# Mean of values for keyless queries in a hash attention: from GpSimd sums and a late addition to TensorE sums and one matmul per head

## The chip, the cores and the metric

The kernel runs on one core of a Trainium2 chip. The metric is the time of one execution on the device, in microseconds, as the median of several runs. The core's engines are TensorE (PE), VectorE (DVE), ScalarE (ACT), GpSimd (POOL) and SyncE (SP), which here mainly issues DMAs. Each engine runs its own instructions strictly in the order in which they stand for it.

## What is computed

Attention over hash buckets comes first: 2 batches of 8 heads, 768 queries and keys, 64 columns per head. A query attends only to the keys whose 6-bit hash equals its own. Where a query has no key in its bucket, all its scores are equal, so its result is the plain mean of all 768 values of the head. The result feeds a mixture of 8 experts.

```python
mask = q_bucket[:, :, :, None] == k_bucket[:, :, None, :]
scores = scale * np.matmul(q, k.transpose(0, 1, 3, 2))
scores = np.where(mask, scores, -1000000000.0)
scores = scores - np.max(scores, axis=-1, keepdims=True)
attn = np.exp(scores)
attn = attn / (np.sum(attn, axis=-1, keepdims=True) + 1e-09)
return np.matmul(attn, v)
...
x = attn_out as (1536, 512); logits = x @ w_gate; one expert per row, capacity 384
out[i] = gate_w[i] * (relu(x[i] @ w1[e]) @ w2[e])
```

## The kernel before

A table named ORDER lists some 900 short steps, written out by hand. The kernel runs them one after the other, each issuing a few instructions, so the table fixes the order on every engine. A step's name may carry an engine after a colon (`:a` ScalarE, `:v` VectorE, `:p` GpSimd, `:vp` one of two each).

The 16 heads (batch times 8 plus head) are handled in two manners. For an **even** head, steps `dS dM dX dY dE d1 f1 f2 dv dw dP dR dQ dN` work on 24 groups of two query tiles: scores on PE (`dS`), the row maximum on DVE (`dM`), its sign and scale (`dX`, `dY`), the exponential on ACT (`dE`), the split into a high and a low part in f16 (`d1` ACT, `dv` DVE and `dw` POOL), a transposing DMA from SP (`f1`, `f2`), the product with the values on PE (`dP`), and the division on DVE (`dR dQ dN`). For an **odd** head, steps `rM rR rF` find all row maxima, `mT mA mD` transpose them and write them by DMA into two rows of the query operand `QB`, and then `rS rE r1 r2 rP` form transposed scores, exponentials, the two parts and the product, three steps per head. The odd head's product accumulates in a PSUM tile of tag `acc`, and `fs` divides it into X.

PSUM tags: `pt` score tiles, `acc` (one buffer), `misc` (one buffer, shared by `mt`, `vb`, `dacc` and others).

Values come in four groups `w` of four heads (HV = 4); a group holds two odd heads. Step `va` takes the largest absolute value, `vT vR vE vB vC` make a power-of-two scale of it on all partitions (`vB` on PE, `vC` on DVE), `v1` writes the high part in f16 with a column of ones beside it, and `v2` the low part.

The mean of an odd head goes another way: `vS` adds the six tiles of raw values on POOL (line 334 once, line 336 four times per group), `vB` sums over partitions with a matmul by ones in f32 (line 977), `vA` copies it, scaled by 1/768, to SBUF on ACT (line 991). `rF` has POOL mark the queries without a key (line 296, `nm`), `nm` multiplies mark and mean (line 401) on POOL or DVE, and `fa` adds that to X after `fs` (line 908).

Of the kernel before, what the change touches and what calls it, by code (L numbers as in the profile page):

```python
# [63 lines left out]
dE1.0 rR3.0 rM4.1 vA1 pl5 rS2.1 vC1 r10 v20.1 rM5.1 rE2.1 v10.2:a dP2 rR5.1 pl2 f10 rM4.0 rM5.0 rR4.1 rS1.1 dR2
v11.3:a v11.0:a rR4.0 dQ2 rR5.0 v20.2 rS1.0 r20:pp rS2.0 pb5 d11 f20 rE1.1 dN2 v21.3 sH7:a pb2 rM3.1 rE1.0 dP0 dS3.0
dv1:v rE2.0 dR0 rR3.1 dQ0 ph4 ph7 dS3.1 sL7 rP0 dw1:p dM3.0 f11 r11 rM8.0 v11.1:a f21 dX3.0 ld6 rF3 dY3.0:a dM3.1 dN0
r21:pp r12 dX3.1 rR8.0 hM2.0 hB2.0 dE3.0 rM7.0 r22:pp rR7.0 dS5.0 dY3.1:a dS4.1 dE3.1 dM5.0 mT3 d13 dS5.1 rP1 mA3
dv3:p dM5.1 hM2.1 dM4.1 dX5.0 dX5.1 f13 mD3 dX4.1 v11.2:a rP2 hB2.1 dY5.1:a dP1 dY5.0:v dw3:v pl4 v21.2 v20.3 dE5.1
pl7 f23 dE5.0 fs1 pb4 rS3.0 v21.0 dR1 dY4.1:a dQ1 dE4.1 fa1:p rE3.0 rS3.1 rM6.1 rR6.1 d15 rE3.1 rM7.1 rM8.1 dN1 rR7.1
rS5.0 dS4.0 rR8.1 dw5:p lT0.0.0 r13 rM6.0 dv5:v rE5.0 dM4.0 lC0.0.0:a dS7.0 dX4.0 dP3 rR6.0 dY4.0:a dE4.0 rS4.1 r23:vp  # L70
dR3 rS5.1 ld9 dQ3 f15 f25 ww2 tb v21.1 pb7 d14 dN3 dM7.0 f14 rE4.1 dX7.0 lM0.0.0 rF5 rE5.1 lv2 lA0.0.0 dw4:p sH6:a
rS4.0 nm3:v lT0.0.1 dv4:v dS7.1 dY7.0:v rE4.0 dM7.1 dX7.1 dS6.1 lC0.0.1:a mT5 sH9:a mA5 dY7.1:v r14 f24 rP3 dM6.1 dP5
dX6.1 dY6.1:v dE7.0 dE7.1 dS6.0 sL6 dR5 dQ5 mD5 d17 dN5 dM6.0 ph6 sL9 hM3.0 dX6.0 r15 r24:pv f17 rS6.0 ld11 dw7:v
# [13 lines left out]
lC0.2.1:a dw12:p dS14.0 nm7:v lM0.2.0 dv12:p mD9 dM13.1 dE13.0 r111 lA0.2.0 dM14.0 ph13 dS14.1 hM5.0 dX13.1 dY13.1:a
rP10 dX14.0 dE13.1 dM14.1 rM16.1 hB5.0 dP11 dX14.1 rR16.1 dR11 dY14.0:a f112 pl13 dQ11 dN11 dE14.0 v22.1 dY14.1:a
v22.2 r211:pp f212 rS12.0 rS13.1 d113 vT3 pl10 pb13 dE14.1 rE12.0 rS12.1 vR3 rP11 rE12.1 dw13:v f113 r112 dv13:p dP12
ld12 pb10 rM18.1 dR12 rS13.0 rE13.1 vE3 d114 dQ12 sH12:a rM15.1 dN12 rR18.1 vB3 f213 rR15.1 rS14.1 vA3 rE13.0 dS15.1  # L90
vC3 r212:pp lM0.2.1 ld15 fs7 wm dM15.1 lA0.2.1 ph12 rS14.0 dP13 dv14:v v13.3:a rE14.1 f114 rM19.0 dR13 dQ13 sL12 rE14.0
sH15:a dw14:p wF dX15.1 dN13 sL15 dY15.1:a dS15.0 rF11 r113 rR19.0 dE15.1 f214 dM15.0 mT11 rP12 mA11 dX15.0 dS17.0
dY15.0:a hM6.1 fa7:v dS17.1 dM17.0 dE15.0 dX17.0 r213:pp hB6.1 d115 r114 dM17.1 rM20.0 hM6.0 rR20.0 dX17.1 dS16.1
hB6.0 dv15:p mD11 ph15 dY17.0:a dY17.1:a dE17.0 lT0.3.1 rP13 lC0.3.1:a v13.1:a dM16.1 dw15:v lT0.3.0 rM19.1 f115
dE17.1 dX16.1 dY16.1:a v22.3 v23.3 r214:vv f215 lC0.3.0:a rS16.0 dP14 vO3 rE16.0 dR14 pl12 dQ14 rS16.1 nm9:v dN14 d117
# [1485 lines left out]
```

## Time and profile before

| What | us |
|---|---|
| Median of three runs (424.79, 429.37, 437.17) | 429.37 |
| The profiled execution | 425.73 |
| Span from first to last instruction in its trace | 423.9 |

The profiled execution is 3.64 us below the median of the runs, and 1.8 us of it lie outside the span. A time worked out from the trace is therefore added to 425.73 and compared with that first. Attention takes the first 250 us or so, the experts most of the rest.

### The profile page before, as it was taken

To read this page: it belongs to the slowest core of one execution; us is meant where nothing else is said; L and a number is where in the kernel's file an instruction comes from. 1 tells how busy PE (TensorE), PEld (TensorE's weight loads), DVE (VectorE), ACT (ScalarE), POOL (GpSimd) and SP (SyncE) were. 2 spreads that over 40 slices of the span, in tenths; PEclk is the share of its full clock that TensorE was granted. 3 is DMA by queue.
4 is the path that set the end of the run, shared out by engine and by line. 5 is a ranking of instruction groups with operands and counts; after the bars stand their busy time and mean duration, and the time that the engine had idled before them with its cause. 6 is when DMAs were issued, how large, how long until landed. Compare 5 with 4: busy or idle time off the path is not lost.

```text
span 423.9 us, 10033 instructions
## 1 busy us (share of the span) xinstructions
PE 392.8 (93%) x3839; PEld 307.0 (72%) x3839; DVE 324.0 (76%) x773; ACT 301.2 (71%) x412; POOL 210.1 (50%) x194
## 2 busy tenths in 40 slices
...
PEclk9999799999999996999999998999999999999998
...
GB/s 205 262 221 133 162 180 168 243 233 180 220 185 191 177 156 208 145 187 226 177 195 207 123 338 275 231 347 359 365 340 286 260 321 283 310 252 46 37 4 38
DMA packets 112400, 89.84 MB, mean 212 GB/s; under 512 B 92226, under 2 KB 94258, under 8 KB 112344
## 3 DMA queue, kind: packets, MB, share of 16 engines
...
q8 instruction: 32, 0.52, 0.5%
...
HBM read 48.37 MB, written 6.88 MB: 130 GB/s over the span
## 4 chain that ended last, share of the span: by engine, by line
issue 32%; PE 22%; DVE 15%; DMA 12%; POOL 8%; ACT 6%; SPq 3%; POOLq 1%; another core or an unknown queue 0%; ACTq 0%; DVEq 0%
PE pt L713 12%; DVE dm L727 4%; PE dacc L791 4%; DMA t<-d 3%; POOL xr L184 3%; DMA QB<-mr 2%; DMA xd<-X 2%; DVE mx L831 2%; POOL y L1352 2%; DVE d L780 2%; ACT p L758 2%; ACT p L862 2%; DMA KB<-bits 2%; PE acc L791 2%; DMA xr<-xd,gix 1%
## 5 line engine op out<-in xcount | busy, mean ns | idle before, releaser
L1352 POOL DMA_INDIRECT y<-y,yix x16 | 18.5, 1158 | 121.1 <-ACT y L1351 110.8
L780 POOL TENSOR_TENSOR p<-p,p 128x768 f16<-128x768 f32 x37 | 63.1, 1726 | 18.2 <-ACT p L866 12.0
L1342 PE MATMUL ph<-x,w1h 128*128 128x224 f16 x448 | 64.9, 259 | 0.0
L713 PE MATMUL pt<-KA,QA 128*128 128x512 f32 x192 | 57.5, 382 | 2.1 <-ACT p L862 0.9
L780 POOL TENSOR_TENSOR d<-p,d 128x768 f16<-128x768 f32 x27 | 46.7, 1740 | 23.0 <-ACT d L766 12.2
L1342 PE MATMUL ph<-x,w1l 128*128 128x224 f16 x224 | 58.1, 259 | 0.0
L713 PE MATMUL pt<-KB,QB 78*128 78x512 f32 x192 | 53.0, 359 | 4.0 <-DMA KB<-bits 1.8
L1260 DVE SCALAR_TENSOR_TENSOR w2l<-r,wsc,w2h 128x1024 f16<-128x1024 f32 x28 | 35.6, 1280 | 25.9 <-ACT w2h L1279 25.9
L831 DVE TENSOR_REDUCE mx<-pt 128x1 f32<-128x768 f32 x48 | 45.0, 951 | 8.5 <-PE pt L713 8.1
L862 ACT ACTIVATE p<-pt,lnb 128x768 f32<-128x768 f32 x48 | 42.4, 894 | 9.1 <-PE pt L713 5.6
L758 ACT ACTIVATE p<-pt,ds 128x768 f32<-128x768 f32 x48 | 46.9, 987 | 2.2 <-POOL d L780 0.5
L727 DVE TENSOR_REDUCE dm<-pt 128x1 f32<-128x768 f32 x48 | 45.3, 948 | 2.7 <-PE pt L713 2.5
L1373 PEld LDWEIGHTS <-hh 128*128 128x128 f16 (+1 forms) x256 | 28.1, 110 | 25.9 <-issue 1.1
L1342 PEld LDWEIGHTS <-w1h 128*128 128x128 f16 x448 | 43.4, 98 | 1.5
L1373 PE MATMUL py<-w2h,hl 128*128 128x512 f16 (+1 forms) x112 | 42.5, 379 | 0.0
L1373 PE MATMUL py<-w2l,hh 128*128 128x512 f16 (+1 forms) x112 | 42.5, 379 | 0.0
L1373 PE MATMUL py<-w2h,hh 128*128 128x512 f16 (+1 forms) x112 | 42.5, 379 | 0.0
L1260 DVE SCALAR_TENSOR_TENSOR w1l<-r,wsc,w1h 128x1024 f16<-128x1024 f32 x28 | 35.9, 1284 | 7.2 <-ACT w1h L1270 7.1
L1305 ACT ACTIVATE hh<-ph 128x224 f16<-128x224 f32 (+2 forms) x69 | 23.0, 341 | 22.7 <-PE ph L1342 20.2
L713 PEld LDWEIGHTS pt<-KB,QB 78*128 78x128 f32 x192 | 31.7, 203 | 10.2 <-DMA QB<-bits 4.5
L766 ACT ACTIVATE d<-p 128x1536 f16<-128x1536 f32 x24 | 35.5, 1480 | 5.0 <-DMA t<-d 2.9
L713 PEld LDWEIGHTS pt<-KA,QA 128*128 128x128 f32 x192 | 31.9, 204 | 8.6 <-ACT p L862 2.1
...
## 6 DMA issues: line engine op xcount, KB each, us to landing
...
```

The lines of the kernel that those rows point to most:

```text
L713: nc.tensor.matmul(t[:, a:z], s[:K, q * 128:(q + 1) * 128], m[:K, a:z], start=(n == 0), stop=(n == 1))
L727: nc.vector.tensor_reduce(out=m, in_=tiles["d", k, t][:, 0:S], axis=AX.X, op=ALU.max, negate=True)
L758: nc.scalar.activation(out=p32_of("dp", k)[:, t], in_=pt_last("d", k, t), func=AF.Exp, scale=s[:, 0:1], bias=s[:, 1:2])
L766: nc.scalar.activation(out=tiles["d1", k], in_=tiles["dp", k], func=AF.Copy)
L780: eng.tensor_tensor(out=out[:, t], in0=p32[:, t], in1=p1[:, t], op=ALU.subtract)
L791: nc.tensor.matmul(a[:, 0:c], p, v, start=first and n == 0, stop=last and n == 2, skip_group_check=True)
L831: nc.vector.tensor_reduce(out=m[:, 0, q:q + 1], in_=pt_last("m", r, t), axis=AX.X, op=ALU.max)
L862: nc.scalar.activation(out=p32_of("rp", r)[:, t], in_=pt_last("e", r, t), func=AF.Exp, scale=0.125, bias=lnb)
L1260: nc.vector.scalar_tensor_tensor(out=lo, in0=r, scalar=sc, in1=hi, op0=ALU.mult, op1=ALU.subtract, accum_out=chk_col())
L1342: nc.tensor.matmul(ph, w[:, k], x2[:, 4 * a + k], start=(n == 0), stop=(n == 11))
L1352: nc.gpsimd.indirect_dma_start(out=view, out_offset=bass.IndirectOffsetOnAxis(ap=yix[:m, j:j + 1], axis=0), in_=y[:m], in_offset=None, bou ...
L1373: nc.tensor.matmul(py[t], h[:, g, c], W2[e, g][w], start=(f == 0 and n == 0), stop=(f == 7 and n == len(ops) - 1))
```

## The change

The four steps `vS`, `vA`, `nm`, `fa`, the second matmul of `vB` and the marking in `rF` go. In their place:

- `uM` (per group): twelve f16 matmuls add the high and low parts of the values of the two odd heads over all 768 keys, with a stationary operand of 12 equal columns, into the `acc` bank (12 rows, 130 columns). `uB` copies that to f16 on ACT, `uK` subtracts this copy from rows 6 to 11 by one matmul, so that they hold the rest, and `uL` spreads the rows on DVE into `sel`, 12 rows by 780 columns, zero wherever the row is not that of the query tile.
- `mN` (per odd head): DVE makes `none`, 12 rows by 128 queries, 32768 where a query has no key and 0 elsewhere, out of the transposed maxima, right behind `mA`. The `misc` buffer is held until then.
- The first `rP` of each odd head starts with one matmul of `none` by `sel` (390 columns), to which the products with the values are then added; `fs` divides all of it.

In the table, `v20.3` and `v21.3` change places, as do `v22.2` and `v22.3`, and `rP18` moves from behind `f218` to behind `dS21.0`. Line numbers of the changed kernel are larger by 13 to 15 in these parts.

```diff
-sH5:a rR2.1 ph2 zp0 rR1.1 vS0 dS2.1 dM2.1 rF1 dS2.0 dX2.1 dM2.0 dS0.1 dX2.0 sL5 dY2.1:a mT1 mA1 vB0 dM0.1 dE2.1
+sH5:a rR2.1 ph2 zp0 rR1.1 dS2.1 dM2.1 rF1 dS2.0 dX2.1 dM2.0 dS0.1 dX2.0 sL5 dY2.1:a mT1 mA1 mN1 vB0 dM0.1 dE2.1
...
-            nc.gpsimd.tensor_scalar(out=nm, in0=mx[g][:, 0], scalar1=-BIG / 2, scalar2=None, op0=ALU.is_lt)
...
-        def v_mean(w):
-            t = vv[w, "raw"].rearrange("p (h a) k d -> p h a k d", a=2)[:, :, 1]
-            a = big.tile([128, HV // 2, D], F32, tag="vsum", name="vsum")
-            nc.gpsimd.tensor_tensor(out=a, in0=t[:, :, 0], in1=t[:, :, 1], op=ALU.add)
-            for k in range(2, NT):
-                nc.gpsimd.tensor_tensor(out=a, in0=a, in1=t[:, :, k], op=ALU.add)
-            vv[w, "sum"] = a
...
-            on().tensor_tensor(out=tmp, in0=nmat.pop(g).unsqueeze(2).to_broadcast([128, NT, D]),
-                                    in1=vv[w, "mean"][:, h // 2:h // 2 + 1].to_broadcast([128, NT, D]), op=ALU.mult)
...
+        def mean_sums(w):
+            if w == 0:
+                mean_const()
+            mean[w] = m = ps.tile([128, NT, D + 1], F32, tag="acc", name="ms")[0:12, 0:HR]
+            for n, x in enumerate(("v1", "v2")):
+                v = vv[w, x].rearrange("p (h a) k d -> p a h k d", a=2)[:, 1]
+                for k in range(NT):
+                    nc.tensor.matmul(m[:, :, 0:D + 1 - n], c12, v[:, :, k], start=(n == 0 and k == 0), stop=False,
+                                     skip_group_check=True)
+
+        def mean_high(w):
+            nc.scalar.activation(out=mb, in_=mean[w], func=AF.Copy)
+
+        def mean_low(w):
+            nc.tensor.matmul(mean[w], d12, mb, start=False, stop=True, skip_group_check=True)
+
+        def mean_rows(w):
+            shape = [12, HR, NT, D + 1]
+            nc.vector.tensor_tensor(out=sel, in0=mean.pop(w).unsqueeze(2).to_broadcast(shape),
+                                    in1=em.unsqueeze(1).unsqueeze(3).to_broadcast(shape), op=ALU.mult)
...
+            def mN(g):
+                none[g] = rot.tile([12, 128], F16, tag="nt", name="nt", bufs=3)
+                nc.vector.tensor_scalar(out=none[g], in0=tiles.pop(("mt", g))[:12, :128], scalar1=-BIG / 2, scalar2=32768.0,
+                                        op0=ALU.is_lt, op1=ALU.mult)
...
+                if r % 3 == 0:
+                    nc.tensor.matmul(a.rearrange("p t d -> p (t d)"), none.pop(g), sel[:, h // 2].rearrange("p t d -> p (t d)"),
+                                     start=True, stop=False, skip_group_check=True)
...
-            def fa(g):
-                b, h = divmod(g, H)
-                xo = X[:, b * NT:(b + 1) * NT, h * D:(h + 1) * D]
-                on().tensor_tensor(out=xo, in0=xo, in1=nmts.pop(g), op=ALU.add)
```

VectorE near 52 us in the trace of before: `v21.3` (line 328, a low part of values of group 1), then `dv1` (line 780), then `dR0` (line 811, which reads the PSUM tile `dacc`).

```order
L821 TENSOR_TENSOR X<-dacc,rsd 128x2x64
L328 SCALAR_TENSOR_TENSOR v_537<-vraw_281,scs,v_536 128x384
L780 TENSOR_TENSOR d_688<-p_516,d_629 128x768
L811 TENSOR_SCALAR rsd<-dacc,scs 128x2
L831 TENSOR_REDUCE mx<-pt 128x1
```

The same place after the change; `v_376` and `v_377` are the two parts of the values of group 0.

```order
L836 TENSOR_TENSOR X<-dacc,rsd 128x2x64
L325 SCALAR_TENSOR_TENSOR v_377<-vraw_234,scs,v_376 128x384
L395 TENSOR_SCALAR d_130<-cs 12x12
L397 TENSOR_TENSOR em<-cs 12x6
L795 TENSOR_TENSOR d_691<-p_503,d_614 128x768
L417 TENSOR_TENSOR sel<-ms,em 12x780
L826 TENSOR_SCALAR rsd<-dacc,scs 128x2
L846 TENSOR_REDUCE mx<-pt 128x1
```

`v20.3` has taken the place of `v21.3`, and two small constants and the spreading into `sel` (`uL0`, line 417) now stand ahead of `dR0`.

Group 2 on ScalarE, near 160 us: the copy of the mean (`vA3`, line 991), then exponentials of odd heads (line 862: `rE13.0`, `rE14.1`, `rE14.0`) and a high part of the values (`v13.3`, line 322).

```order
L686 ACTIVATE KA_111<-raw_2619 128x768
L991 ACTIVATE mean<-vb 128x128
L862 ACTIVATE p_2636<-pt,lnb 128x768
L322 ACTIVATE v_2679<-vraw_1657,scs 128x6x64
L862 ACTIVATE p_2747<-pt,lnb 128x768 x2
L686 ACTIVATE KA_114<-raw_2688 128x768
```

The same place after the change.

```order
L701 ACTIVATE KA_111<-raw_2619 128x768
L882 ACTIVATE p_2636<-pt,lnb 128x768
L410 ACTIVATE mb<-ms 12x130
L319 ACTIVATE v_2676<-vraw_1669,scs 128x6x64
L882 ACTIVATE p_2758<-pt,lnb 128x768 x2
L701 ACTIVATE KA_114<-raw_2685 128x768
```

The copy for the mean has moved from ahead of `rE13.0` to behind it, and it reads `ms`, the sums of `uM2`.

Group 2 on TensorE, a little further on: scores `rM19.0`, scores `dS15.0`, the transposed maxima `mT11` (line 842) and the first product of `rP12`.

```order
L713 MATMUL pt<-KB_123,QB_118 128x512
L713 MATMUL pt<-KB_123,QB_118 128x256
L713 MATMUL pt<-KA_112,QA_107 128x512
L713 MATMUL pt<-KA_112,QA_107 128x256
L713 MATMUL pt<-KB_122,QB_117 128x512
L713 MATMUL pt<-KB_122,QB_117 128x256
L842 MATMUL mt<-cs,mx 12x128
L791 LDWEIGHTS p_2579
```

The same place after the change.

```order
L728 MATMUL pt<-KB_123,QB_118 128x512
L728 MATMUL pt<-KB_123,QB_118 128x256
L413 LDWEIGHTS d_130
L413 MATMUL ms<-mb,d_130 12x130
L728 MATMUL pt<-KA_112,QA_107 128x512
L728 MATMUL pt<-KA_112,QA_107 128x256
L728 MATMUL pt<-KB_122,QB_117 128x512
L728 MATMUL pt<-KB_122,QB_117 128x256
L857 MATMUL mt<-cs,mx 12x128
L907 LDWEIGHTS nt
L907 MATMUL acc<-sel,nt 128x390
L806 LDWEIGHTS p_2579
```

`uK2` stands between the two score steps and needs ScalarE's copy, and the product of `none` and `sel` now opens `rP12`.

## Rows read from the trace of the kernel before

**Rows 1.** The page: engine, busy us (share of the span) xinstructions, then clock by slice

```profile
PE 392.8 (93%) x3839; PEld 307.0 (72%) x3839; DVE 324.0 (76%) x773; ACT 301.2 (71%) x412; POOL 210.1 (50%) x194
...
PEclk9999799999999996999999998999999999999998
```

**Rows 2.** Windows: us, busy time (xinstructions) of PE, PEld, DVE, ACT, POOL, clock, DMA share

```profile
75.00:100.00 25.00, 23.84 (x311) 20.02 (x310) 23.39 (x48) 23.49 (x28) 19.78 (x15) 1.00 1.11 227
275.00:300.00 25.00, 25.00 (x180) 17.75 (x178) 21.10 (x53) 19.33 (x28) 6.77 (x4) 1.00 1.07 356
```

**Rows 3.** Groups by shape, removed work: line engine op out<-in xcount | busy us, mean ns

```profile
L336 POOL TENSOR_TENSOR vsum<-vsum,vraw 128x128 f32<-128x128 f32 x16 | 8.0, 503 | 1.3
...
L908 POOL TENSOR_TENSOR X<-X,nmt 128x384 f32<-128x384 f32 x5 | 5.3, 1063 | 10.5 <-DVE X L902 10.5
...
L401 POOL TENSOR_TENSOR nmt<-nm,mean 128x384 f32<-128x384 f32 x5 | 4.1, 826 | 0.0
...
L908 DVE TENSOR_TENSOR X<-X,nmt 128x384 f32<-128x384 f32 x3 | 2.8, 942 | 0.0
...
L401 DVE TENSOR_TENSOR nmt<-nm,mean 128x384 f32<-128x384 f32 x3 | 2.4, 814 | 0.0
...
L977 PE MATMUL vb<-vsum,cs 128*128 128x128 f32 x8 | 2.0, 326 | 0.0
...
L991 ACT ACTIVATE mean<-vb 128x128 f32<-128x128 f32 x4 | 1.0, 260 | 0.0
```

**Rows 4.** Groups by shape again, operations like those that are added

```profile
L821 DVE TENSOR_TENSOR X<-dacc,rsd 128x128 f32<-128x128 f32 x24 | 6.9, 287 | 0.4
...
L902 DVE TENSOR_TENSOR X<-acc,rsr 128x384 f32<-128x384 f32 x8 | 4.5, 558 | 0.3
...
L850 DVE SCALAR_TENSOR_TENSOR mr<-mt,mh 12x128 fp32r<-12x128 f32 x8 | 2.2, 278 | 0.3
```

**Rows 5.** Timeline near 52 us: start, us, engine, line, op, out<-in xcount [idle before <-releaser]

```profile
51.78 0.52 PE L713 MATMUL pt<-KA,QA 128*128 128x512 f32 x2
...
52.09 0.95 DVE L780 TENSOR_TENSOR d<-p,d 128x768 f16<-128x768 f32 x1
...
52.49 1.27 PE L791 MATMUL dacc<-v,t 128*128 128x65 f16 x36
...
53.80 0.22 DVE L811 TENSOR_SCALAR rsd<-dacc,scs 128x2 f32<-128x2 f32 x1 [0.77 <-PE dacc L791]
```

**Rows 6.** Chain that ended last, near 63 us: start us, us, what

```profile
63.15 4.29 DMA QB<-mr
```

**Rows 7.** The chain near 105 and near 220 us

```profile
105.52 4.40 DMA KB<-bits
...
218.08 1.00 POOL X L908
...
220.30 4.39 DMA t<-d
```

**Rows 8.** Windows of 2 us near 160 us

```profile
158.00:160.00 2.00, 0.81 (x6) 0.47 (x4) 0.00 (x0) 0.98 (x2) 0.35 (x1) 1.00 0.36 79
160.00:162.00 2.00, 1.96 (x9) 1.61 (x9) 1.55 (x6) 2.00 (x5) 1.73 (x1) 0.59 1.03 199
162.00:164.00 2.00, 2.00 (x17) 1.60 (x17) 2.00 (x3) 0.87 (x2) 1.83 (x3) 0.50 0.98 277
```

**Rows 9.** Timeline near 162 us

```profile
160.38 0.16 DVE L982 COPY scs<-vb 128x4 f32<-128x4 f32 x1 [2.43 <-ACT mean L991]
...
161.03 0.61 ACT L322 ACTIVATE v<-vraw,scs 128x384 f16<-128x384 f32 x1
...
162.25 1.64 POOL L780 TENSOR_TENSOR d<-p,d 128x768 f16<-128x768 f32 x1 [0.17 <-POOL QB L931]
...
162.44 2.27 DVE L780 TENSOR_TENSOR d<-p,d 128x768 f16<-128x768 f32 x1
...
163.57 0.90 ACT L862 ACTIVATE p<-pt,lnb 128x768 f32<-128x768 f32 x1 [1.13 <-PE pt L713]
```

More of the change, by code (lines that the diff above doesn't have):

```diff
@@ L64 @@
[L64 to L73, printed above, removed]
@@ new lines @@
+dY2.0:a dE2.0 dS0.0 ph3 d12 vC0 hM1.1 ph5 dX0.1 dS1.1 dY0.1:v ld7 mD1 dM0.0 ld4 v10.0:a dX0.0 f12 hB1.1 vO0 hM0.1
+dE0.1 dY0.0:a dw2:p dE0.0 rS0.0 v10.1:a hB0.1 hM0.0 rE0.0 dv2:p va1 dS1.0 hB0.0 rS0.1 vT1 sH4:a dM1.1 pl3 rE0.1 sL4
+f22 vR1 v10.3:a d10 dM1.0 dX1.1 vE1 pb3 hM1.0 hB1.0 dv0:p vB1 dY1.1:a rM3.0 dX1.0 v20.0 dY1.0:a dE1.1 dw0:v dE1.0
+rR3.0 rM4.1 pl5 rS2.1 vC1 r10 v20.1 rM5.1 rE2.1 v10.2:a dP2 rR5.1 pl2 f10 rM4.0 rM5.0 rR4.1 rS1.1 dR2 v11.3:a v11.0:a
+rR4.0 dQ2 rR5.0 v20.2 rS1.0 r20:pp rS2.0 pb5 d11 f20 rE1.1 dN2 v20.3 sH7:a pb2 uM0 rM3.1 uB0 rE1.0 dP0 uK0 dS3.0 dv1:v
@@ new lines @@
+uL0 rE2.0 dR0 rR3.1 dQ0 ph4 ph7 dS3.1 sL7 rP0 dw1:p dM3.0 f11 r11 rM8.0 v11.1:a f21 dX3.0 ld6 rF3 dY3.0:a dM3.1 dN0
+r21:pp r12 dX3.1 rR8.0 hM2.0 hB2.0 dE3.0 rM7.0 r22:pp rR7.0 dS5.0 dY3.1:a dS4.1 dE3.1 dM5.0 mT3 d13 dS5.1 rP1 mA3 mN3
+dv3:p dM5.1 hM2.1 dM4.1 dX5.0 dX5.1 f13 mD3 dX4.1 v11.2:a rP2 hB2.1 dY5.1:a dP1 dY5.0:v dw3:v pl4 v21.2 v21.3 dE5.1
+pl7 f23 dE5.0 fs1 pb4 rS3.0 v21.0 dR1 dY4.1:a dQ1 dE4.1 rE3.0 rS3.1 rM6.1 rR6.1 d15 rE3.1 rM7.1 rM8.1 dN1 rR7.1 rS5.0
+dS4.0 rR8.1 dw5:p lT0.0.0 r13 rM6.0 dv5:v rE5.0 dM4.0 lC0.0.0:a dS7.0 dX4.0 dP3 rR6.0 dY4.0:a dE4.0 rS4.1 r23:vp dR3
@@ L87 @@
[L87 to L95, printed above, removed]
-ld14 rP14 lM0.3.0 v23.1 rE16.1 pl15 rS15.0 rR19.1 lA0.3.0 lM0.3.1 v13.0:a dE16.1 pb12 fs9 rS15.1 dw17:v fa9:v r116
+mN9 dX12.1 dY12.1:a dM13.0 rM15.0 rR15.0 dX13.0 hM5.1 r210:pp dE12.1 d112 dS13.1 dY13.0:a hB5.1 ph10 lT0.2.1 f211
```

117 lines of the change are left out of this document (64 added, 53 removed).

## The prediction

> **What bounds the kernel now.** I read the page first. TensorE is busy for 392.8 of 423.9 us, 93%, VectorE for 76%, GpSimd for 50% [rows 1]. The windows by stage then separate two kernels. In the experts, from 275 us on, TensorE is busy for 25.00 of 25 us; nothing that the change touches runs there, except that it may start later. In attention, 75 to 100 us, TensorE has 23.84, VectorE 23.39 and GpSimd 19.78 us of 25 [rows 2]: three engines that hand work to each other in a fixed order, with one to six us of slack each. So a busy us saved on GpSimd, the one with most slack, is not a us saved, while a us put in the order of TensorE or VectorE is one unless a transfer is waited for later on. Third, the chain that ended last: it passes through DMAs of 4.3 to 4.4 us (maxima into `QB` at 63.15, hash bits into `KB` at 105.52, transposed parts at 220.30) [rows 6, 7]. Behind such a DMA a delay stays only if it was there before the DMA was issued.
>
> **What goes.** On GpSimd: 8.0 us of sums (line 336), 5.3 of `fa`, 4.1 of `nm` [rows 3], 17.4 us in the three largest groups of an engine that is idle for half the span. On VectorE 2.8 + 2.4 = 5.2 us, on TensorE 2.0, on ScalarE 1.0 us [rows 3]. What is worth something of that:
> - VectorE's three heads of 1.76 us each (0.94 + 0.81). Most stand where TensorE or ScalarE end nearly as late; I take half of one pair, 0.9 us, between 0 and 5.2.
> - `vC3` on VectorE waits 2.43 us for ScalarE's `vA3` [rows 9], since both read the bank that `vB3` wrote. That wait goes. But right behind it TensorE has been waiting for a DMA (busy 0.81 us of the 2 from 158 on) [rows 8], and that stays. I take 0.3, between 0 and 0.9.
> - GpSimd's `fa11` stands on the chain at 218.08 for 1.00 us, and behind it is the issue of the transposing DMA at 220.30 [rows 7]. By the table SP has another transposing DMA (`f120`) and a weight load (`wp0`) to issue ahead of that one, whatever GpSimd does: 0.
> - Fewer moments in which VectorE and GpSimd run together. At 162.44 VectorE's product takes 2.27 us while GpSimd's stands at 162.25 for 1.64 [rows 9], and the same instruction takes 0.95 us at 52.09 [rows 5]. The 17.4 us would have to meet VectorE in an instruction that is slowed, on the chain. I take 1.0, from 0 to 7 (a third of the 17.4 us, and the 1.32 us that this one instruction lost).
>
> **What comes, in each odd head.** `mN` reads 12 x 128 like line 850, 0.28 us each [rows 4], so 2.2 us on VectorE for eight, behind `mA` and ahead of row maxima that wait. The matmul of `none` by `sel` has 390 columns. The 36 matmuls of a product, 2328 columns of the same width of data, take 1.27 us [rows 5], 0.55 ns per column, so 0.21 us, or 1.7 us for eight. `rP` on TensorE has little to wait for, so most of the 1.7 delays TensorE, but only a part of both lies where the chain runs. Together 3.9 us, of which I take 1.0; bounds 0 and 3.9.
>
> **What comes, in each group.** `uM` has 1548 columns in twelve matmuls, by the same price 0.84 us at full clock. `uB` is like `vA`, 0.26 [rows 3]. `uK` is one matmul of 130 columns, 0.1 us. `uL` makes 780 columns out of PSUM: lines 821 and 902 take 287 ns for 128 and 558 for 384 columns [rows 4], 1.06 ns a column and 0.15 at the start, so 0.98 us. The work by itself is 1.9 us a group, 7.6 us in all. Worse is that the four are a chain across PE, ACT, PE and DVE, each with other work queued behind it.
>
> *Group 0, near 52 us.* `uM0` waits for `v20.3`, which VectorE ends just ahead of 52.09, while TensorE is free for it at 51.78, where it starts `rM3.1` in before [rows 5]: 0.3 to 0.4 us of wait. So TensorE is late by 0.4 + 0.84 = 1.2 us when `dP0` (52.49 in [rows 5]) starts. `uK0` is queued behind `dP0` and `uL0` on VectorE behind `uK0`; `dR0`, which VectorE ran at 53.80 as soon as `dP0` ended [rows 5], comes after 1.2 + 0.1 + 0.98, 2.3 us late. All of VectorE is behind it: `rR3.1`, `dX3`, `dN0`, and the maxima that go ahead of the DMA at 63.15 [rows 6]. This lies before the issue, so it stays. I take 2.3; the least is 0.8 (if slack on the way takes TensorE's wait and half of the spreading), the most 2.8.
>
> *Group 1, near 99 us.* VectorE spreads for 0.98 us and no longer runs one `fa` and `nm` pair of 1.76; TensorE gets 0.9 us more. At 105.52 the chain goes over to a 4.40 us DMA for hash bits [rows 7], for which TensorE waits whatever came before. I take 0.1, from 0 to 0.9.
>
> *Group 2, near 162 us.* The clock granted here is half: 0.59 and 0.50 in the windows from 160 and 162, after the wait in which TensorE is busy for 0.81 us of 2 [rows 8]. `uM2` stands behind `rS14.0` and takes 1.7 us rather than 0.84. `uB2` stands on ScalarE ahead of `v13.3` and two exponentials, the last of which runs at 163.57 for 0.90 us, right behind the end of `rS14.0` [rows 9]. It can't start until `uM2` ends, near 163.5 + 1.7 = 165.2, so that ScalarE ends at 165.2 + 0.26 + 0.61 + 2 times 0.90 = 167.9, 3.4 us late. `rM19.0` waits for the bank that they free, `uK2` for `rM19.0`, `uL2` for `uK2`, and on VectorE a sign and scale (`dX15.1`) waits for `uL2`, 4.2 us late if nothing is absorbed. Some is, since the stretch is loose with the clock at half. I take 2.8, from 1.5 to 4.2.
>
> *Group 3, near 216 us.* `uL3` and `mN15` (0.98 + 0.28) stand ahead of `dM22.0`, and `rP18` moves back by one score step, so that TensorE doesn't wait for `sel`. The DMA at 220.30 follows an SP queue that is full, and is waited for to 224.69 [rows 7]. I take 0.8, from 0 to 1.5.
>
> **The sum.** Added: 2.3 + 0.1 + 2.8 + 0.8 + 1.0 = 7.0. Gone: 0.9 + 0.3 + 1.0 = 2.2. Net +4.8 us, 430.5 for an execution like the profiled one at 425.73. The median of the three runs is 3.64 above the profiled one and the lowest 0.9 below it; between them, with a third of the distance, the forecast is 431. A measurement of this kernel can tell some 2% from no change, 8.5 us; the forecast lies inside that.
>
> **Rivals.**
>
> *GpSimd's relief decides (faster).* The place is all of attention: 17.4 us less on GpSimd, and with them the slowed VectorE instructions go and GpSimd's products (lines 780) start earlier. For it: the 2.27 us against 0.95 [rows 9, 5]. Against it: GpSimd is idle half of the time [rows 1], and the transfers behind its products are issued by SP in order. With the 7 us bound for the relief, the rest of the gains at their upper bounds (5.2 + 0.9) and 7.0 added, the sum is -6.1: 420. It takes over if a third of the removed GpSimd time is met by VectorE.
> [...]
>
> *The chain of four steps drops the clock (slower).* TensorE waits near 52 us for `uM0`, and near 165 us for the bank behind `uB2`. If those waits lower its granted clock as the wait at 158 to 160 us did, to 0.50 for about 6 us [rows 8], each costs some 3 us more, as half of 6; two of the 40 slices show such a fall in before [rows 1]. With 4.2 for group 2, 2.8 for group 0 and 2 times 3: 7.0 + 1.4 + 0.5 + 6.0 - 2.2 = +12.7, 438. It decides from a wait of about 1.2 us on TensorE, as the 158 us one was; group 0's is 0.4, and group 2 is at half clock already, so one of the two drops at most is likelier: 434 to 436.
>
> *Nothing is left over (same).* The three 4.3 us DMAs [rows 6, 7] and SP's queue absorb all but what is ahead of the first one. Then +2.3 from group 0 and less than the gains from the rest: 426 to 428. For it: behind each such DMA TensorE waits for its landing; against it: the delays in groups 0 and 2 come before the issue of the next DMA.
>
> *The change does not take its work off GpSimd* can be ruled out: its steps are no longer in the table.
>
> **How the numbers follow.** My forecast, some 3 to 8 us more, has 0.50; nothing left over 0.22; the clock or a longer chain 0.18; relief 0.10. The range reaches from the relief case's upper half, 422, to 440, one above the clock case with 438. Faster by over 2% needs 8.5 us, more than the relief case's 6.1 gives from the median: 0.07 with what I can't see. Slower by over 2% needs the clock case or both bounds, 0.18. Within 2%: 0.75.
>
> **What would show it.** GpSimd's busy time about 188, VectorE's within 2 us of 324, TensorE's 395 or more at the same clock. At 52 us `dR0` should run about 2.3 us later than 53.80, and the DMA at 63.15 by about the same. At 162 us `uM2` at 1.7 us, `uB2` ending near 165.5, and the exponential of 163.57 near 167. The 2.43 us wait of `vC3` should be gone. I am wrong if the DMA at 63.15 starts no later, if the slowed VectorE products become rare, or if a window of half clock appears near 53 us or ends later than 168 us.

## The result, and the profile after

The changed kernel takes 433.72 us (median of 20 runs, 429.87 to 443.32); the kernel before took 427.32 us in the runs beside it (20 runs). The ratio is 1.0138, 95% interval 1.0108 to 1.0169: slower by 6 us, inside 2%. Some executions of each kernel are longer (of the changed one four of the 20, 436.54 to 443.32 us); the ratios leave these out, the medians do not, and the profiles of `e2_sums`, `e3_again` and `e3_hybrid`, which are such executions, are not used. The profiled execution took 433.79 us, its span is 432.0, 8.1 us more than that of before.

The page of the changed kernel: busy time by engine, then the granted clock in 40 slices.

```profile
PE 397.4 (92%) x3891; PEld 309.5 (72%) x3891; DVE 326.9 (76%) x781; ACT 302.4 (70%) x412; POOL 189.8 (44%) x157
...
PEclk8568999989999999899999999999999999999998
```

GpSimd has lost 20.3 us of work against [rows 1], VectorE has gained 2.9 and TensorE 4.6. The gain on VectorE is not added work: in a second profile of this kernel (`e1_again` below) VectorE is busy for 322.2 us, 1.8 less than in before. The clock row is new too: the low slices stand at the start now.

The windows of the stages that stood in [rows 2] (time, then busy time of PE, PEld, DVE, ACT, POOL).

```profile
75.00:100.00 25.00, 20.91 (x282) 17.17 (x282) 22.07 (x40) 20.36 (x23) 15.83 (x11) 0.93 0.96 215
275.00:300.00 25.00, 23.76 (x198) 18.83 (x197) 22.29 (x70) 19.53 (x35) 6.93 (x4) 1.00 1.05 320
```

From 75 to 100 us TensorE is busy for 20.91 us of 25 where it was for 23.84. None of the added steps explains this loss; the reason comes below.

The groups by shape of the added operations.

```profile
L417 DVE TENSOR_TENSOR sel<-ms,em 12x780 f16<-12x780 f32 x4 | 3.8, 956 | 2.9 <-PE ms L413 2.8
...
L907 PE MATMUL acc<-sel,nt 12*128 12x390 f16 x8 | 2.8, 354 | 0.0
...
L870 DVE TENSOR_SCALAR nt<-mt 12x128 f16<-12x128 f32 x8 | 2.2, 269 | 0.0
L406 PE MATMUL ms<-v,c 128*12 128x130 f16 x24 | 2.1, 220 | 0.0
L406 PE MATMUL ms<-v,c 128*12 128x128 f16 x24 | 2.0, 220 | 0.0
...
L410 ACT ACTIVATE mb<-ms 12x130 f16<-12x130 f32 x4 | 1.1, 269 | 4.8 <-PE ms L406 4.8
...
L413 PE MATMUL ms<-mb,d 12*12 12x130 f16 x4 | 0.9, 216 | 0.4 <-ACT mb L410 0.4
```

The spreading takes 0.956 us (forecast 0.98), the marks 0.269 (0.28), the copy 0.269 (0.26). The records of matmuls overlap: one of `uM` is 0.22 us long, and twelve in a row take 0.86 us (forecast 0.84), as the next rows show. So the 0.354 us of the product of `none` are not its price either: the next matmul starts 0.26 us after it at 54.48 (forecast 0.21).

The timeline of the changed kernel at group 0, near 50 us.

```profile
49.93 0.86 PE L406 MATMUL ms<-v,c 128*12 128x130 f16 x12
...
50.82 0.27 ACT L410 ACTIVATE mb<-ms 12x130 f16<-12x130 f32 x1 [0.29 <-PE ms L406]
...
52.73 0.22 PE L413 MATMUL ms<-mb,d 12*12 12x130 f16 x1
...
52.98 0.96 DVE L417 TENSOR_TENSOR sel<-ms,em 12x780 f16<-12x780 f32 x1 [1.68 <-PE ms L413]
...
53.87 0.20 DVE L826 TENSOR_SCALAR rsd<-dacc,scs 128x2 f32<-128x2 f32 x1
...
62.95 0.79 SPq L874 DMA_DIRECT2D QB<-mr  x1
```

`uM0` takes 0.86 us, `uK0` stands behind `dP0`, VectorE waits 1.68 us for it and spreads for 0.96, and `dR0` runs at 53.87. By the absolute time this is as late as in [rows 5] (53.80), but the changed kernel had come to this place 1.94 us ahead (before's clock was granted at 0.50 from 42 to 46 us), so `dR0` lost 2.0 us. The DMA that stood at 63.15 in [rows 6] starts at 62.95, so it lost 1.7.

The timeline at group 2.

```profile
164.07 0.15 DVE L989 COPY scs<-vb 128x4 f32<-128x4 f32 x1
...
166.69 0.85 PE L406 MATMUL ms<-v,c 128*12 128x130 f16 x12
...
167.58 0.27 ACT L410 ACTIVATE mb<-ms 12x130 f16<-12x130 f32 x1 [2.03 <-PE ms L406]
...
168.26 1.66 ACT L882 ACTIVATE p<-pt,lnb 128x768 f32<-128x768 f32 x2
...
170.33 0.96 DVE L417 TENSOR_TENSOR sel<-ms,em 12x780 f16<-12x780 f32 x1 [1.12 <-PE ms L413]
...
171.22 0.13 DVE L747 TENSOR_SCALAR ds<-dm 128x1 f32<-128x1 f32 x1
```

`vC3`, which waited 2.43 us in [rows 9], waits for nothing. `uM2` runs at full clock, in 0.85 us and not 1.7. ScalarE waits 2.03 us for it.

To place the losses I took the start of each TensorE step in one profile less its start in the profile of before (for `lM0.2.1` that of its fourth matmul of six), and from that how much later the step at the far side of a place is than the one at its near side. These are worked out from the timelines, in us.

| Kernel (profiled execution) | group 0, `rS2.0` to `rM8.0` | group 1, `rM9.0` to `rM12.0` | group 2, `lM0.2.1` to `hM6.1` | group 3, `dS22.0` to `rS21.1` | sum | near 89, `rS6.1` to `rM11.0` | last product |
|---|---|---|---|---|---|---|---|
| changed, first profile | 1.60 | 1.36 | 1.77 | 1.87 | 6.60 | 4.93 | 255.6 |
| changed, `e1_again` | 1.60 | 1.34 | 1.78 | 1.86 | 6.58 | 0.04 | 251.2 |
| `e1_removed`, no mean | 0.01 | 0.30 | -0.95 | 0.01 | -0.63 | -0.01 | 246.6 |
| `e2_move` | 0.01 | -0.20 | -0.88 | 0.26 | -0.81 | 1.39 | 248.9 |
| `e2_none` | 0.37 | 0.18 | -1.86 | 0.84 | -0.47 | 1.53 | 246.5 |
| `e1_chain` | 1.25 | 1.01 | 0.11 | 1.51 | 3.88 | 0.00 | 251.8 |
| `e3_half` | 1.26 | 1.01 | 1.63 | 1.54 | 5.44 | 1.54 | 251.2 |
| `e2_twice` | 2.29 | 2.05 | 3.23 | 2.55 | 10.12 | 5.14 | 261.8 |
| `e1_late` | 2.01 | 1.35 | 2.18 | 1.86 | 7.40 | 1.50 | 255.3 |
| `e4_fill` | 1.60 | 1.36 | 1.86 | 1.88 | 6.70 | 1.37 | 254.8 |

The last column is the end of the last attention product from the span's start; in before it is 246.9. Both profiles of the changed kernel lose the same 6.6 us at the four groups. Only the first loses 4.93 near 89 us.

Two cautions. In group 2 before runs at half clock [rows 8], so a number there is a difference of two clocks too; counted from the first matmul of `lM0.2.1` it is lower by 0.4 us (by 0.2 in `e3_half` and `e2_twice`). And at `rS2.0`, ahead of group 0, all these kernels stand 1.1 to 3.9 us ahead of before. Much of that lead is gone by the end: `e1_removed` is 3.92 us ahead at `rS2.0` and 0.3 at the last product. So the sum of the four places is what is lost there and not the difference of the ends.

### The profile page after: what moved, and what is told of

It is laid out like the page before. It is cut to its first block, busy times and chain, and to the rows that moved or that the text cites. A ratio compares the mean times of both kernels' runs of the same rounds, so it can differ in the third digit from the quotient of the medians.

```text
span 432.0 us, 10111 instructions
## 1 busy us (share of the span) xinstructions
PE 397.4 (92%) x3891; PEld 309.5 (72%) x3891; DVE 326.9 (76%) x781; ACT 302.4 (70%) x412; POOL 189.8 (44%) x157
## 4 chain that ended last, share of the span: by engine, by line
PE 33%; issue 29%; DVE 14%; DMA 13%; POOL 5%; ACT 4%; SPq 1%; POOLq 1%; another core or an unknown queue 0%; DVEq 0%; ACTq 0%
PE pt L728 15%; PE dacc L806 4%; DMA t<-d 4%; PE acc L806 4%; DVE dm L742 3%; POOL xr L184 3%; DVE d L795 3%; PE pb L272 2%; DMA xd<-X 2%; DMA xr<-xd,gix 2%; DVE mx L846 2%; POOL y L1366 1%; ACT p L882 1%; PE ph L1356 1%; PE py L1387 1%
## 5 line engine op out<-in xcount | busy, mean ns | idle before, releaser
L795 POOL TENSOR_TENSOR p<-p,p 128x768 f16<-128x768 f32 x37 | 62.0, 1692 | 30.1 <-ACT p L886 17.5
L795 POOL TENSOR_TENSOR d<-p,d 128x768 f16<-128x768 f32 x27 | 49.2, 1835 | 44.8 <-DMA t<-d 32.1
L728 PE MATMUL pt<-KA,QA 128*128 128x512 f32 x192 | 58.8, 390 | 2.9 <-ACT p L882 1.6
```

Of the source, the lines that this page charges most:

```text
L728: nc.tensor.matmul(t[:, a:z], s[:K, q * 128:(q + 1) * 128], m[:K, a:z], start=(n == 0), stop=(n == 1))
L795: eng.tensor_tensor(out=out[:, t], in0=p32[:, t], in1=p1[:, t], op=ALU.subtract)
```

## The experiments

The theories: A, the added steps stand ahead of other work on TensorE, ScalarE and VectorE (A1: TensorE's time for the sums by itself; A2: the waits along the four steps), and B, the changed timing makes VectorE's and GpSimd's two-operand products meet. All ratios are to before, run on the same chip, with 95% intervals.

**e1_again.** The changed kernel, unchanged, for a second profile.

> The changed kernel once more, for a second profile. Theory A (queues: the added steps stand ahead of other work on TensorE, ScalarE and VectorE, and that is the loss): the time is 1.2 to 1.6% over before, and the four places are late as in the first profile, by about 1 us near 52, 0 to 2.5 near 165 and 2 near 220. Theory B (meeting: the changed timing lets two-operand products of VectorE and GpSimd meet near 88 to 92 us, where VectorE's two take 4.7 us rather than 1.9): the 3.3 us jump near 89 us stands in this profile too. If the jump is missing and the time is the same, the jump was one execution's chance.

431.7 us, ratio 1.0048 (0.999 to 1.0106), below the 1.2 to 1.6% that theory A expected. The four places are late as in the first profile, and the jump near 89 us is missing. The rows on both sides of it, in the first profile:

```profile
87.62 3.95 POOL L795 TENSOR_TENSOR p<-p,p 128x768 f16<-128x768 f32 x2 [0.69 <-POOL p L795]
87.67 4.72 DVE L795 TENSOR_TENSOR d<-p,d 128x768 f16<-128x768 f32 x2
...
93.03 1.17 PE L272 MATMUL pb<-KA,ST 128*56 128x384 f32 x4 [3.17 <-DVE bits L281]
```

and in the second:

```profile
86.56 1.82 DVE L795 TENSOR_TENSOR d<-p,d 128x768 f16<-128x768 f32 x2
...
87.41 4.11 POOL L795 TENSOR_TENSOR p<-p,p 128x768 f16<-128x768 f32 x2 [2.66 <-issue]
```

In the first, GpSimd's two products (`r25`) start at 87.62, VectorE's two (`dw7`, `dv7`) at 87.67; VectorE then takes 4.72 us and TensorE waits 3.17 us for hash bits behind it. In the second VectorE's first product starts 0.85 us ahead of GpSimd's, and its two take 1.82. That order alone doesn't decide: in `e1_late` VectorE's first is ahead by 0.82 us too, and the two take 3.3. There it is VectorE's second product that meets GpSimd's first one:

```profile
86.67 1.65 POOL L795 TENSOR_TENSOR p<-p,p 128x768 f16<-128x768 f32 x1 [2.65 <-issue]
86.72 2.42 DVE L795 TENSOR_TENSOR d<-p,d 128x768 f16<-128x768 f32 x1
```

The same two in `e1_chain`:

```profile
88.29 0.95 DVE L794 TENSOR_TENSOR d<-p,d 128x768 f16<-128x768 f32 x1
88.34 2.42 POOL L794 TENSOR_TENSOR p<-p,p 128x768 f16<-128x768 f32 x1 [2.60 <-issue]
```

With 0.05 us between the starts, the one that starts second takes 2.42 us, and the other 0.95 (VectorE) or 1.65 (GpSimd). In the first profile above VectorE's products start 0.05 us behind GpSimd's, and the two take 4.72 us. But in `e1_again` GpSimd's product starts first by the records, 0.02 us ahead (87.41, VectorE's second at 87.44), and is the slow one with 2.49 us. What slows one of the two is not shown.

It is a race that goes either way: VectorE's two products take 1.8 us in before, `e1_removed`, `e1_again` and `e1_chain`, and 3.3 to 3.5 in `e1_late`, `e2_move`, `e2_none`, `e3_half`, `e4_fill` and `e2_twice`, so both outcomes come with the change and without it. The 4.72 us came in one profile alone, and whether the change makes the bad outcome likelier is not shown. Theory B fell as an account of what the four groups lose: that is the same with the jump and without it.

**e1_removed.** Before, with the mean of values left out altogether: two of the lines that go are below, and from the table go `vS0` to `vS3`, `vA0` to `vA3` and every `nm` and `fa`.

```diff
-            nc.gpsimd.tensor_scalar(out=nm, in0=mx[g][:, 0], scalar1=-BIG / 2, scalar2=None, op0=ALU.is_lt)
...
-                nc.tensor.matmul(t[:, 128:128 + n_mean], cs[:, C_ONE:C_ONE + 128], ...
...
```

> The kernel before, with the mean of values left out altogether: no sums on GpSimd, no second matmul of vB, no copy, no marks, no product and no addition to X; nothing is added and no step is moved. Theory A: what was taken away is worth 2.2 us (0 to 4), so 423 to 427 where before is 427.3, -0.5%. Theory B: the same work removed shifts GpSimd, so that this kernel is no faster or even slower than before by up to 3 us, with a jump near 89 us. If GpSimd's relief were worth a lot, it would be 7 us or more faster.

429.64 us, ratio 0.9998 (0.9931 to 1.0064). No gain shows from all that the change takes away: without it, and with nothing put in its place, the time is that of before, to within 0.7% (3 us).

**e1_chain.** The sums, the copy, the low part and the spreading stay; the marks and the product with them go, so the mean is added to nothing. The other seven `mN` go like `mN1` below.

```diff
-mT1 mA1 mN1 vB0
+mT1 mA1 vB0
...
-                if r % 3 == 0:
-                    nc.tensor.matmul(a.rearrange("p t d -> p (t d)"), none.pop(g), sel[:, h // 2]...
```

> The changed kernel without the eight mN and without the eight matmuls of none by sel (the mean is summed and spread but never added to a result). Theory A: 1 us less than the changed kernel by the forecast's term, at most 3.9, so +0.8 to +1.2% over before. Theory B: the timing shifts by a few tenths of a us per head, the products near 89 us may or may not meet, and the time changes by 3 us or more if they don't.

431.0 us, 1.0051 (0.9993 to 1.0109), the changed kernel beside it 1.0048, so the whole time does not tell them apart. At groups 0 and 1 it is 0.35 and 0.33 us less late than the changed kernel, about one product of `none`. At group 2 it loses 0.11 where the changed kernel loses 1.78. The windows there, first of `e1_again`:

```profile
166.00:168.00 2.00, 1.43 (x7) 0.66 (x7) 2.00 (x5) 1.77 (x3) 1.32 (x3) 0.92 1.10 157
168.00:170.00 2.00, 2.00 (x38) 2.00 (x37) 1.78 (x6) 1.82 (x3) 1.82 (x2) 0.50 1.22 254
170.00:172.00 2.00, 2.00 (x12) 1.65 (x10) 0.54 (x1) 1.94 (x3) 2.00 (x2) 0.73 0.28 61
```

and of `e1_chain`:

```profile
166.00:168.00 2.00, 1.67 (x9) 0.99 (x7) 1.19 (x4) 1.38 (x3) 1.25 (x5) 1.00 1.13 182
168.00:170.00 2.00, 1.76 (x40) 1.74 (x41) 2.00 (x5) 2.00 (x3) 1.77 (x2) 1.00 1.10 241
170.00:172.00 2.00, 1.93 (x12) 1.34 (x11) 1.75 (x6) 1.94 (x4) 2.00 (x2) 1.00 0.49 93
```

In the first TensorE is busy for 1.43 of the 2 us from 166 and the clock then goes to 0.50; in the second it is busy for 1.67 and the clock stays at 1.00. The products of `rP12`, 36 matmuls, show the price, first in `e1_again`, then in `e1_chain`:

```profile
167.99 2.15 PE L806 MATMUL acc<-v,p 128*128 128x65 f16 x36
168.35 1.25 PE L805 MATMUL acc<-v,p 128*128 128x65 f16 x36
```

From their start to that of `hM6.1` the one takes 3.27 us and the other 2.10, 1.2 of the 1.67 us by which the two differ at this place; the other 0.5 us stand just ahead, where the product of `none` is left out.

**e1_late.** The four steps stand later in groups 0 and 2.

```diff
-dv1:v uL0 rE2.0 dR0 rR3.1 dQ0 ph4
+dv1:v rE2.0 dR0 rR3.1 dQ0 uL0 ph4
-rS14.0 uM2 dP13 dv14:v uB2 v13.3:a rE14.1 f114 rM19.0 uK2 ... uL2 sL12 rE14.0 ... dS15.0 rF11 r113 rR19.0
+rS14.0 dP13 uM2 dv14:v v13.3:a rE14.1 f114 rM19.0 ... rE14.0 uB2 ... dS15.0 uK2 rF11 r113 uL2 rR19.0
```

> The changed kernel with uL0 behind dR0, rR3.1 and dQ0, and in group 2 with uM2 behind dP13, uB2 behind the two exponentials rE14.1 and rE14.0, uK2 behind dS15.0 and uL2 behind dX15.1, dN13 and rF11. Theory A: the 2.3 and 2.8 us of groups 0 and 2 shrink to the work itself, some 1 us each, so 2.5 to 3 us faster than the changed kernel, +0.7% over before. Theory B: no more than 1 us faster, and the jump near 89 us stays.

434.67 us, 1.0121 (1.006 to 1.0182). Not faster, where theory A had it 2.5 to 3 us faster than the changed kernel. Group 0 loses 2.01 and group 2 2.18, both more than in the changed kernel. Moving the steps behind other work did not pay: `rP0` and `rP12` need `sel`, and TensorE now waits 0.36 and 0.84 us for it, where in `e1_again` it waits for it at neither. In group 2 `dP13`, which now stands ahead of `uM2`, waits 1.89 us for a DMA besides. The windows there:

```profile
162.00:164.00 2.00, 0.76 (x6) 0.43 (x4) 0.38 (x2) 1.69 (x3) 0.73 (x1) 1.00 0.94 237
164.00:166.00 2.00, 1.36 (x38) 1.31 (x39) 1.06 (x2) 0.00 (x0) 1.24 (x1) 1.00 1.00 235
168.00:170.00 2.00, 1.16 (x15) 0.56 (x14) 1.57 (x2) 2.00 (x2) 2.00 (x2) 1.00 1.26 283
```

TensorE is idle here for longer than ahead of the drop in `e1_again`, the clock stays at 1.00 (until 180 us), and the place loses 2.18 us all the same.

**e2_twice.** The sums done twice over.

```diff
-            for n, x in enumerate(("v1", "v2")):
+            for again in range(2):
+                for n, x in enumerate(("v1", "v2")):
```

> The changed kernel with the sums of uM done twice over (the second pass starts afresh, so the result is the same): 48 more matmuls, 0.87 us per group as the profiles show it. Theory A1 (TensorE's own time for the sums delays all that follows): 4 x 0.87 = 3.5 us over the changed kernel, +0.8%, each place with a jump of 1.7 us in TensorE's steps rather than 0.88. Theory A2 (only the waits along the four-step chain cost, or later DMAs take the delay up): +1 us or less. Theory B (GpSimd and VectorE meeting): no direction, a jump near 89 us or none.

448.11 us, 1.045 (1.0382 to 1.0518), far more than the 0.8% that was expected over the changed kernel. The place of `uM0`:

```profile
49.21 1.54 PE L407 MATMUL ms<-v,c 128*12 128x130 f16 x24
```

It takes 1.54 us, 0.68 more than in the changed kernel, and TensorE's next step is 0.68 us later. The four places together lose 10.12 us, 3.54 more than in `e1_again`. That is A1's 3.5 in part by luck: groups 0, 1 and 3 lose 0.69, 0.71 and 0.69 more, the added sums themselves, and group 2 loses 1.45 more, since the clock had fallen to 0.50 ahead of `uM2` there and its 24 matmuls took 2.77 us. The span is 18.4 us longer than that of `e1_again`. Of this 5.1 lie near 89 us (the products met, and the clock stood at 0.50 behind it), 1.9 elsewhere in attention, and 7.9 in the experts. All six runs lie at 446.94 us or more, so the 10 us or more beyond A1's 3.5 are not the chance of one execution; where they come from is open.

**e2_sums.** The sums alone: `uB`, `uK`, `uL`, `mN` and the product of `none` are left out, so the mean is summed and used nowhere.

> The changed kernel with the sums of uM alone: no uB, uK, uL, no mN and no product of none and sel, so the mean is summed and used nowhere. Theory A1: the jumps of 0.88 us stay and the time lies within 1 us of the kernel with the whole chain and without mN (+0.5% over before). Theory A2: the jumps near 165 and the half clock behind them go (PE no longer waits for uB2 and uL2), 2 us faster than that kernel, about the time of before.

431.25 us, 1.0034 (0.9991 to 1.0077). Between before and the whole chain, and not to be told from either, so this run doesn't decide between A1 and A2.

**e2_move.** No mean at all, with the three moves in the table alone (`v20.3` with `v21.3`, `v22.2` with `v22.3`, `rP18` behind `dS21.0`).

> The kernel without any mean, with only the three moves in the table added (v20.3 with v21.3, v22.2 with v22.3, rP18 behind dS21.0). Theories A1 and A2: the moves cost nothing by themselves but rP18's, 0 to 1 us: the time of the kernel without any mean, within 1 us. If the moves were a cost of their own, 2 us or more, seen near 52 or near 216 us.

430.85 us, 1.0009 (0.9957 to 1.0061). The moves cost nothing that shows; `rP18`'s is 0.25 us at its place.

**e2_none.** The marks and their products stay, `sel` is zero throughout, `uM`, `uB`, `uK`, `uL` are left out; the mean added is zero.

```diff
             def mN(g):
+                if not none:
+                    nc.gpsimd.memset(sel, 0.0)
```

> The changed kernel without uM, uB, uK and uL: sel is set to zero once, and the eight mN and the eight products of none and sel stay, so that the mean added is zero. The forecast's term for these sixteen instructions is 1.0 us (0 to 3.9): 1 us over the kernel without any mean. Theories A1 and A2: +0.2%, no half clock near 170 us beyond that which the kernel before has near 162.

431.83 us, 0.9981 (0.9921 to 1.0041). The sixteen instructions cost nothing that the time shows; at groups 0 and 3 they leave 0.37 and 0.84 us (the latter with the moved `rP18`).

This kernel has no half clock in group 2 either (1.00 in every window of 2 us from 160 to 180). Its -1.86 there beside the 0.11 of `e1_chain` gives what `uM2`, `uB2`, `uK2` and `uL2` cost at equal clock: 2.0 us at least, since only `e2_none` has the product of `none` besides.

**e3_again, e3_half, e3_hybrid.** The changed kernel a third time, and two ways to give TensorE less to sum.

> The changed kernel once more, as the measure for the other two on this chip: +0.5 to +1.4% over before by the two comparisons so far. In the profile the two products of VectorE near 88 us take 1.8, 3.3 or 4.7 us by which of VectorE and GpSimd starts first, at no fixed value.

434.76 us, 1.0134 (1.0073 to 1.0195). The three comparisons of the same kernel lie at 1.0138, 1.0048 and 1.0134.

`e3_half` sums the high parts alone, so the mean lacks its low part.

```diff
-            for n, x in enumerate(("v1", "v2")):
+            for n, x in enumerate(("v1",)):
```

> The changed kernel with uM adding the high parts of the values alone, six matmuls a group in place of twelve (the mean lacks its low part). Theory A1 (TensorE's time for the sums is what delays): 0.43 us less per group, 1.7 us less than the changed kernel. Theory A2 (the four-step chain and its waits): within 0.5 us of it. Theory C, from the doubled sums, which cost 16 us and not 3.5: each us of sums is worth several, so 4 us or more less.

435.67 us, 1.0183 (1.0126 to 1.0239), no faster than the changed kernel beside it, so theory C, by which it was to be 4 us or more faster, is out. Its place of `uM0`:

```profile
50.75 0.52 PE L406 MATMUL ms<-v,c 128*12 128x130 f16 x6
```

It takes 0.52 us, and the four places lose 5.44 us, 1.1 less than in `e1_again`; the last product ends at 251.2 in both, with 1.5 of it due to the race near 89 us in this one alone. But its span is 9.1 us longer than `e1_again`'s, all of it in the experts. The timeline shows where:

```profile
276.02 12.72 SPq L169 DMA_DIRECT2D r<-w  x4
...
289.42 0.55 PE L1356 MATMUL ph<-x,w1h 128*128 128x224 f16 x2 [5.97 <-DMA x<-xs]
```

The same issue in `e1_again`:

```profile
277.00 4.82 SPq L169 DMA_DIRECT2D r<-w  x4
```

SP spends 12.72 us from the first to the end of the last of four weight loads, where it spent 4.82. Most of that is a wait ahead of the fourth; SP's own waits, first in `e3_half` from 274 to 290 us, then in `e1_again` from 275 to 284:

```profile
SPq L169 <- DMA x<-xs: 7.7, 1, 7.7
SPq L169 <- DMA x<-xs: 2.8, 1, 2.8
```

By the trace it waits for a transposing DMA of inputs (`x<-xs`) that was issued at 271.66 and landed at 288.36; in `e1_again` the same one was issued at 271.68 and landed at 281.43. TensorE's 5.97 us are for the next of these DMAs, issued at 273.83 and landed at 289.38. So both wait for landings that come some 7 us later, and SP's issuing is not what takes the time. `e2_twice` has that wait too (5.2 us), `e1_removed` 2.4 us, `e4_fill` 0.85; before, the two profiles of the changed kernel and `e1_late` have none. Why these DMAs land so much later in some executions is open.

`e3_hybrid` puts GpSimd's sums back in idle stretches of GpSimd, and `uM` becomes one f32 matmul over them: `vS`, five additions on GpSimd as before, and `uS`, a multiplication by the scale, stand behind `dv3`, `sL11` and `dv15` in groups 1 to 3.

```diff
-                    nc.tensor.matmul(m[:, :, 0:D + 1 - n], c12, v[:, :, k], start=(n == 0 and k == 0), stop=False, ...
+            nc.tensor.matmul(m, c12, vv[w, "sum"], start=True, stop=False, skip_group_check=True)
...
```

> The changed kernel with GpSimd's sums put back in idle stretches of GpSimd (five additions and one scaling a group) and uM made one f32 matmul of 130 columns over them in place of twelve f16 ones; uB, uK, uL, mN and the product of none and sel stay. Theory A1: uM falls from 0.85 to about 0.3 us, so some 2.2 us less than the changed kernel, about +0.2% over before; the copy, the low part and the spreading are short enough to be hidden. Theory A2: the chain across PE, ACT, PE and DVE is the cost, and the time is that of the changed kernel. If taking work off GpSimd had been worth anything, this kernel would be slower than the changed one.

437.72 us, 1.0135 (1.0061 to 1.021), where the changed kernel beside it has 1.0134. A1's 2.2 us did not show, but the interval is 3 us to each side, so this tells little.

**e4_fill.** Eight matmuls more in group 2, put into TensorE's waits by two steps `uW2` of four each.

```diff
-uM2 dP13 dv14:v uB2 ... dS15.0 rF11
+uM2 dP13 uW2 dv14:v uB2 ... dS15.0 uW2 rF11
...
+                nc.tensor.matmul(whole[w][0:12, 2:4], c12, v[:, :, k], start=True, stop=True, ...)
```

> The changed kernel with eight matmuls of 130 columns more in group 2, four behind dP13 and four behind dS15.0, where TensorE waits 0.4 and 0.6 us for ScalarE and VectorE; their result is read by nothing. Theory D (in group 2 the loss is not the waits but the half clock that follows them: 0.50 in the 2 us from 168, 1.8 us lost, against 0.1 us lost in the kernel without mN and none, whose clock stayed 1.00): the windows behind the place stay at 1.00 and the lateness gained there is 0.6 us or less, 1.2 us less than in the changed kernel. Theory A1 (TensorE's time): 8 x 0.07 = 0.6 us more where they don't fit into the waits, and the half clock stays. In the whole time 0.3% either way, not to be told apart.

437.82 us, 1.0249 (1.0165 to 1.0333). The windows:

```profile
166.00:168.00 2.00, 1.25 (x35) 1.01 (x31) 1.01 (x3) 0.71 (x3) 2.00 (x1) 1.00 1.05 228
168.00:170.00 2.00, 1.10 (x6) 0.74 (x6) 0.00 (x0) 2.00 (x4) 0.72 (x4) 1.00 1.08 176
170.00:172.00 2.00, 1.82 (x13) 1.06 (x13) 1.95 (x5) 1.26 (x3) 1.56 (x1) 1.00 1.19 258
```

The clock stayed at 1.00, as theory D had it (this execution comes to the place 2.6 us later than `e1_again`, and the windows up to 180 us are at 1.00 too), and the place lost 1.86 us all the same. The timeline tells why:

```profile
164.87 0.85 PE L412 MATMUL ms<-v,c 128*12 128x130 f16 x12
...
166.86 0.40 PE L396 MATMUL ms<-v,c 128*12 128x130 f16 x4
...
167.29 0.27 ACT L416 ACTIVATE mb<-ms 12x130 f16<-12x130 f32 x1 [3.50 <-PE ms L396]
...
168.90 0.61 PE L734 MATMUL pt<-KA,QA 128*128 128x512 f32 x2 [1.65 <-ACT p L888]
```

`uB2` now waits 3.50 us for the four extra matmuls, which write the same PSUM tile, and TensorE waits 1.65 us for ScalarE behind it. The experiment put a wait where it took the clock drop away, so what the drop costs in group 2 rests on the one comparison of `e1_again` with `e1_chain`. It is not the whole loss: `e1_late` and `e4_fill` lose 2.18 and 1.86 us there with no drop.

No version that computes the mean is faster than before, and since the kernel without any mean is as fast as before to within 0.7%, none of this kind can be by much.

## Why the prediction was right or wrong

The time was forecast as 431 us in 422 to 440, inside 2%, and was 433.72; the loss as 4.8 us, and was 6.4 between the medians. The sign and the main reason held: no gain shows from GpSimd's relief, and four short chains across three engines cost more than what they replace. That the time came so close is in part luck, since terms missed in both directions. The terms:

- **What goes: 2.2 us.** None of it shows: `e1_removed` has 0.9998, no gain at all in the middle of its interval, though the interval still admits 3 us. `vC3`'s wait [rows 9] did go; a gain from it was not seen.
- **Group 0: 2.3 us.** It is 1.60 on TensorE; 2.0 for `dR0`, 1.7 at the DMA's issue. The mechanism (`uM0`, then `uL0` ahead of `dR0`) is as told; the 0.3 to 0.4 us of wait for `v20.3` did not come.
- **Group 1: 0.1 us.** This step failed. The DMA at 105.52 [rows 7] was to take up all but 0.1, 0.9 at most; the place lost 1.34 and 1.36 in two profiles, of which only part was given back at the landing near 110 us (`e1_again` is 0.86 late ahead of it, 0.46 behind). The 1.76 us of an `fa` and `nm` pair that VectorE no longer runs there were worth nothing (`e1_removed`, without the pair, is 0.30 later here), and TensorE's own 0.86 us of sums stayed.
- **Group 2: 2.8 us.** 1.78, 2.7 against `e1_removed`, at least 2.0 at equal clock (`e1_chain` less `e2_none`). By the parts the account was wrong: `uM2` ran at full clock in 0.85 us; the half clock came behind the chain instead of ahead of it. The last exponential ended at 168.26 + 1.66 = 169.92, 5.45 later than in before [rows 9], where `rS14.0` ahead of it was 3.90 later: it lost 1.6 us, not 3.4.
- **Group 3: 0.8 us.** 1.87: the 0.86 us of sums, 0.4 of waiting for `uB3`, 0.2 of `uK3`, the product of `none` (0.3) and the moved `rP18` (0.25 in `e2_move`) all stand in TensorE's order, and the place lost more than the forecast let the transfer at 220.30 [rows 7] take up.
- **Each odd head: 1.0 us.** `e2_none` costs nothing that shows in the time; about 0.35 us at the first head of a group (`e1_again` less `e1_chain` at groups 0 and 1).

So 6.0 us were forecast for the groups and 6.6 came, by smaller terms in 0 and 2 and larger ones in 1 and 3. `e2_twice` shows what a good part of these is: 0.68 us of sums added to each place adds 0.7 us to three of them (and 1.45 to group 2, by the clock). `e3_half` fits (0.34 us of sums less in each, 1.1 us less in all). That is A1, in the places. In the whole time A1 is not shown to that size: twice the sums cost 13 to 17 us more than the changed kernel and not 3.5, half of them gained nothing, and the intervals of `e2_sums`, `e3_half` and `e3_hybrid` don't tell these three from the changed kernel.

Of the rivals, GpSimd's relief at its 6.1 us is ruled out by `e1_removed`. Nothing left over is ruled out by the interval of the main comparison (1.0108 at least), though not by that of `e1_again` alone (0.999 to 1.0106). The clock rival has something: a half clock near 170 us follows the chain in both profiles of the changed kernel, where the forecast named a window of half clock later than 168 us as a sign against it. But before has one at the same place, ahead of it [rows 8], so a drop is moved and not added, and `e1_chain`, `e2_none`, `e1_late` and `e4_fill` have none there. Nor did its condition, a wait of about 1.2 us on TensorE, hold: the waits ahead of the drop in `e1_again` are 0.44 and 0.57 us, and `e1_late` waits 1.89 us in the same stretch and keeps its clock.

Of the other signs, GpSimd (189.8 us, about 188 forecast) and TensorE (397.4) came as said; VectorE's 326.9 is 0.9 us beyond the 2 us that were allowed it, by the slowed products. The DMA at 63.15 [rows 6] started no later by its time, 62.95, which was to mean that the forecast was wrong; it lost 1.7 us only beside steps that had come 1.94 us ahead. The 8.1 us between the two first profiles hold 4.93 near 89 us that came and went with the race, and hide a drop of the clock at 42 to 46 us that before had and this one had not.
